# Sign of decoded weights by ScalarE, a first fold without group sum, and a first step in two halves, in a fused attention and expert kernel

## The chip, the cores and the metric

One core of a Trainium2 chip. The metric is the device time of one execution in microseconds, as a median of runs. All engines are named as in the profile: PE is TensorE, DVE VectorE, ACT ScalarE, POOL GpSimd, SP the queue that issues transfers.

## The reference

Causal attention (4 batches, 12 heads, 448 positions, head size 64), a soft mixture of 8 experts with 4 slots each, and a last feed-forward part of which this change touches the product:

```python
# x: 1792 tokens x 768, from the attention
c = softmax(x @ phi, axis=1)                 # 1792 x 32
x = c @ slot_out                             # slot_out: 32 x 768, from the experts
h = x @ w_in                                 # w_in: 768 x 2048
g = h * np.cos(h)
out = g @ w_out                              # w_out: 2048 x 768
```

`w_in` and `w_out` are float64 arrays; everything is computed in float32.

## The kernel before

Attention and experts come first, in orders written out by hand (HEAD, ORDER, TAIL and a loop over 48 pieces of expert weights, lines 799 to 857). Then the last part, which this document is about.

**Fold.** Since x = c @ slot_out, h is c @ (slot_out @ w_in). So `w_mm` (L868) multiplies the 32 slots with a chunk of 128 columns of `w_in`, in six products over the 768 rows (`soT`, the transposed slots, against the decoded item `fwi`). These six are spread over four groups of 32 rows of a PSUM bank, so that `w_4` (L884, ScalarE copy), `w_rep` (L887, a product with a 0/1 matrix that adds the four groups) and `w_s` (L890, ScalarE copy) follow. `w_d` (L894, VectorE) makes the residue for the low part, and the chunk lies in `WS`. GRP lists the chunks that are folded together: chunks 0 and 1 alone, the others in pairs.

**Steps.** A step is a block of tokens (three of 512, one of 256) and a chunk of 128 hidden columns: 64 steps, in the order of SEQ. Each runs `t_h` (H, TensorE product L910), `t_y` (Y, ScalarE, rounding to whole turns, L914), `t_r` (R, VectorE, L917), `t_s` (S, ScalarE, sine, L920), `t_g` (G, VectorE, times h, L923), `t_k` (K, ScalarE, the high part of g, L926) and `t_l` (L, the low part of g, on GpSimd, or on VectorE for the steps in LE, L929). Then come the products B that multiply g with `w_out`: six groups of three (high by high, high by low, low by high; `back`, L936 to L938), 12 products in the last block (`back3`, L964 to L966), and for step 0 in the order `back0` (L946): all six high by high, all six high by low, all six low by high.

**Decoding.** The float64 weights are loaded as pairs of 32-bit words, one item of 768 KB per chunk of `w_in` ("i") and `w_out` ("o"), 32 items; the words lie in four raw buffers. `dec_a` (L732, ScalarE) multiplies the high words, read as float32, by 2^-112, which moves the exponent; `dec_l` (L735, VectorE) shifts the low words right by 29; `dec_h` (L739, VectorE) shifts the high words left by 3 and ors them in, by which the sign falls out; `dec_s` (L743, VectorE) takes the sign bit from the high words and ors it in. For `w_out`, `up_part` (L754, ScalarE) and `lo_part` (L767, VectorE or GpSimd, by VE) split the item in a high and a low part. Three items are decoded in the expert part, by `next_piece` (L774), 29 by the planner's order.

**Order.** A planner (L994 to L1170) gives each operation a cost, what it depends on and a due time (`key`), and writes out one fixed order per engine. KEYS shifts the due times of single operations, LA says how long an engine may hold out for a more urgent one, and VE and LE fix the engine of some operations. It also puts filler products (`keep_warm`, L540) on TensorE while the chain to the first step runs.

In the expert part each piece's products are at L829 or L844, followed for some pieces by three filler products; after each group of four pieces a copy (L848), two transposes (L853, in `bank[6]`) and a copy to `soT` (L854).

Of the kernel before, what the change touches and what calls it, by code (L numbers as in the profile page):

```python
# [33 lines left out]
LA = 0.4  # L34
# [14 lines left out]
VE = {1: 'D', 10: 'P', 11: 'P', 12: 'P', 15: 'D', 6: 'P', 7: 'D'}  # L49
LE = {10: 'D', 11: 'D', 20: 'D', 25: 'D', 41: 'D', 47: 'D', 6: 'D', 8: 'D'}  # L50
# [152 lines left out]
def moe_stack_kernel(ctx: ExitStack, tc: tile.TileContext, qk, v, cst, phi, w1, w2, w_in, w_out, out):  # L203
# [526 lines left out]
    def dec_a(j):  # L730
        w = rawv(j)
        ACT.activation(w[:, :, 1].bitcast(F32), w[:, :, 1].bitcast(F32), AF.Copy, scale=2.0 ** -112)  # L732
# [4 lines left out]
    def dec_h(j):  # L737
        fi = it_f(j).bitcast(I32)
        DVE.scalar_tensor_tensor(fi, rawv(j)[:, :, 1], 3, fi, op0=ALU.logical_shift_left, op1=ALU.bitwise_or)  # L739

    def dec_s(j):
        fi = it_f(j).bitcast(I32)
        DVE.scalar_tensor_tensor(fi, rawv(j)[:, :, 1], -2147483648, fi, op0=ALU.bitwise_and, op1=ALU.bitwise_or)  # L743

    def decode(j):
        dec_a(j)
        dec_l(j)
        dec_h(j)
        dec_s(j)
# [20 lines left out]
    npc = [0]  # L770

# [27 lines left out]
    with tc.manual_schedule():  # L799
# [19 lines left out]
        for g in range(2):  # L819
# [17 lines left out]
            for n in range(3):  # L837
                sb = bank[4 + n % 2]
                for qd in range(4):
                    w = next_piece().rearrange("p (c j f) -> p c j f", c=2, j=4)  # L840
                    for c in range(2):
                        kc = 2 * qd + c
                        for j in range(4):
                            PE.matmul(sb[32 * j:32 * j + 4, 0:256], lhsT=hT[:, kc, 4 * j:4 * j + 4], rhs=w[:, c, j, :],  # L844
                                      start=(kc == 0), stop=(kc == 7))
                    if 42 <= npc[0] < 48:
                        keep_warm(3)
                ACT.activation(so, sb[:, 0:256], AF.Copy)  # L848
# [59 lines left out]
    def t_h(s, hb):  # L908
        blk, fc = seq[s][:2]
        PE.matmul(hb[:, 0:n_(s)], lhsT=WS[0:96, 128 * fc:128 * fc + 128], rhs=CT[:, TOK[blk]:TOK[blk + 1]], start=True, stop=True)  # L910

    def t_y(s, hb):

        ACT.activation(y_(s).bitcast(I32), hb[:, 0:n_(s)], AF.Identity, bias=b_q, scale=1.0 / (2.0 * math.pi))  # L914

    def t_r(s, hb):
        DVE.scalar_tensor_tensor(y_(s), y_(s).bitcast(I32), -2.0 * math.pi, hb[:, 0:n_(s)], op0=ALU.mult, op1=ALU.add)  # L917

    def t_s(s):
        ACT.activation(y_(s), y_(s), AF.Sin, bias=b_h, scale=1.0)  # L920

    def t_g(s, hb):
        DVE.tensor_tensor(y_(s), hb[:, 0:n_(s)], y_(s), ALU.mult)  # L923

    def t_k(s):
        ACT.activation(g_(s)[0], y_(s), AF.Copy)  # L926

    def t_l(s, eng):
        eng.tensor_tensor(g_(s)[1], y_(s), g_(s)[0].bitcast(F32), ALU.subtract)  # L929
# [70 lines left out]
    for j, (k_, c) in enumerate(items):  # L1000
# [3 lines left out]
        else:  # L1004
# [11 lines left out]
            task(("h", j), dict(D=.88), [("a", j), ("l", j)], key - 1.4, True)  # L1016
            task(("s", j), dict(D=.95), [("h", j)], key - 1.3, True)
# [7 lines left out]
    for q, grp in enumerate(GRP):  # L1025
        key = need[grp[0]] - 1.5
        n = len(grp)
        task(("wm", q), dict(T=.14 + .22 * (n + 1)), [("s", 2 * c) for c in grp] + [("w4", q - 2) if q >= 2 else None, ("so",)], key - .8)
        task(("w4", q), dict(A=.15 + .11 * n), [("wm", q)] + [("wr", q - 2) if q >= 2 else None], key - .7)
        task(("wr", q), dict(T=.1 + .22 * n), [("w4", q)], key - .6)  # L1030
        task(("ws", q), dict(A=.15 + .11 * n), [("wr", q)], key - .5)
# [6 lines left out]
    for s, (blk, fc, first, last) in enumerate(seq):  # L1038
        w = n_(s) / 512.0
        task(("H", s), dict(T=.02 + .22 * w), [("wd", qof[fc]), ("H", s - 1) if s else None], s - 3)  # L1040
        task(("Y", s), dict(A=.08 + .52 * w), [("H", s)] + [("K", s - 3), ("L", s - 3)] * (s >= 3), s - 2.6)
# [3 lines left out]
        task(("K", s), dict(A=.1 + .46 * w), [("G", s), ("B", s - 4, nu(s - 4) - 1) if s >= 4 else None], s - 1.7)  # L1045
        task(("L", s), dict(D=.07 + .55 * w) if LE.get(s) == "D" else dict(P=.07 + 1.3 * w), [("K", s)], s - 1.5, True)
        if s == 0:
            task(("B", 0, 0), dict(T=1.4), [("K", 0), ("u", 0)], .0)
            task(("B", 0, 1), dict(T=1.4), [("B", 0, 0), ("v", 0)], .1)
            task(("B", 0, 5), dict(T=1.4), [("B", 0, 1), ("L", 0)], .2)  # L1050
        for m in range(nu(s)):
            if s == 0:
                if last:
                    task(("F", s, m), dict(D=.61) if m % 2 == 0 else dict(A=.5), [("B", 0, 5)], s + .2 + m / 10)
                    pb[m] = ("F", s, m)
                continue
            pv_ = ("B", s, m - 1) if m else (("B", s - 1, nu(s - 1) - 1) if s else None)
            if blk == 3:
                task(("B", s, m), dict(T=(.68, .68, .73)[m]), [("K", s), ("L", s), ("u", fc), ("v", fc), pv_, *([pb.get(x) for x in ((0,), (2,), (1, 3))[m]] if first else [])], s + m / 10)
# [3 lines left out]
            task(("B", s, m), dict(T=.01 + .67 * w), [("K", s), ("L", s), ("u", fc), ("v", fc), pv_, pb.get(m) if first else None], s + m / 10)  # L1063
# [23 lines left out]
    CHN = [("wm", 0), ("w4", 0), ("wr", 0), ("ws", 0), ("wd", 0), ("H", 0), ("Y", 0), ("R", 0), ("S", 0), ("G", 0), ("K", 0), ("B", 0, 0)]  # L1087
# [24 lines left out]
    while len(done) < len(T):  # L1112
# [3 lines left out]
        for e in free:  # L1116
# [40 lines left out]
            if t[0] in ("G", "wd"):  # L1157
                hbf[hbo[("H" if t[0] == "G" else "wm", t[1])]] = fin + .1
# [9 lines left out]
        if not moved:  # L1168
# [4 lines left out]
    run = dict(ld=ld, a=dec_a, l=dec_l, h=dec_h, s=dec_s, u=up_part, S=t_s, K=t_k, B=lambda s, m: (back3 if seq[s][0] == 3 else back if s else back0)(s, m))  # L1173
    run.update(H=lambda s: t_h(s, bk(("H", s))), Y=lambda s: t_y(s, bk(("H", s))), R=lambda s: t_r(s, bk(("H", s))),
               G=lambda s: t_g(s, bk(("H", s))))
    for nm, fn in (("wm", w_mm), ("w4", w_4), ("wr", w_rep), ("ws", w_s), ("wd", w_d)):
        run[nm] = lambda q, fn=fn: fn(q, bk(("wm", q)))
    with tc.manual_schedule():
        for _, _, t, e in plan:
# [7 lines left out]
            elif t[0] == "L":  # L1187
                t_l(t[1], ENG[e])
# [68 lines left out]
```

## Time and profile before

| | us |
|---|---|
| median of 3 runs | 509.07 (507.99 to 509.58) |
| profiled execution | 508.61, its span 506.8 |
| TensorE busy | 479.2 (95% of the span) |
| VectorE busy | 361.6 (71%) |
| ScalarE busy | 306.7 (61%) |
| GpSimd busy | 176.3 (35%) |

The profile is of one execution. Busy times are of single engines; "idle before" of an instruction is the time in which its engine had nothing to run, with what ended it. TensorE's weight loads (PEld) overlap its products; a matmul's end is modelled, so the start times of two matmuls tell more than their durations.

### The profile page before, as it was taken

The page shows a single profiled execution, that of the slowest core. Times are in us where ns is not written, and L with a number is a line of the kernel's source. Part 1 is how long each engine was busy: PE and PEld are TensorE (multiplying, and loading weights), DVE is VectorE, ACT ScalarE, POOL GpSimd, SP SyncE. Part 2 cuts the span into 40 slices and gives each one's busy share as a digit, 9 for nine tenths or more (in the row PEclk, how much of TensorE's full clock was granted, in tenths as well). Part 3 has the DMA queues.
Part 4 walks back from the last instruction along what each step waited for, and adds up shares of the span by engine and source line. Part 5 has one row for each costly group of instructions (what it writes and reads, how often), then busy time and mean ns, then how long its engine had stood idle before and what let it go on. Part 6 is the DMA issues. An engine that isn't in the chain of part 4 may idle for free.

```text
span 506.8 us, 11358 instructions
## 1 busy us (share of the span) xinstructions
PE 479.2 (95%) x4304; PEld 345.1 (68%) x4304; DVE 361.6 (71%) x913; ACT 306.7 (61%) x734; POOL 176.3 (35%) x261
## 2 busy tenths in 40 slices
PE   8999999999998988788999999999999999999996
PEld 5766666666666333246777768777777878888885
DVE  4798889889885530054989999999979786455241
ACT  4998899899892210123877674567457565643361
POOL 2655555555551000000562132514327534312231
PEclk9999999999999999989999999999999999999999
DMA  6488888788867999998352542324252102023101
GB/s 202 121 289 294 285 296 310 276 291 307 292 239 281 407 420 415 423 420 352 124 188 62 188 147 104 117 94 163 63 174 78 58 4 94 32 80 120 51 0 63
DMA packets 23942, 100.38 MB, mean 198 GB/s; under 512 B 2768, under 2 KB 6352, under 8 KB 17744
## 3 DMA queue, kind: packets, MB, share of 16 engines
q1 hardware_dynamic: 23888, 99.66, 53.6%
q8 instruction: 34, 0.56, 0.4%
q14 instruction: 20, 0.16, 0.1%
HBM read 94.14 MB, written 5.51 MB: 197 GB/s over the span
## 4 chain that ended last, share of the span: by engine, by line
PE 40%; DVE 13%; DMA 11%; issue 3%; POOL 2%; ACT 2%; POOLq 0%; ACTq 0%; SPq 0%; DVEq 0%
DMA w<-in_w_dram 11%; PE bank L936 8%; PE bank L938 8%; PE bank L937 8%; PE bank L965 2%; PE bank L964 2%; PE bank L966 2%; PE bank L910 2%; DVE zscr L923 2%; PE bank L829 2%; DVE zfa L735 1%; POOL zg L929 1%; PE bank L540 1%; DVE zscr L917 1%; DVE zps L984 1%
## 5 line engine op out<-in xcount | busy, mean ns | idle before, releaser
L929 POOL TENSOR_TENSOR zg<-zscr,zg 128x512 fp32r<-128x512 f32 (+1 forms) x56 | 74.7, 1338 | 233.5 <-ACT zg L926 121.3
L936 PE MATMUL bank<-zg,zhl 128*128 128x512 f32 x282 | 112.2, 398 | 0.0
L938 PE MATMUL bank<-zg,zhl 128*128 128x512 f32 x282 | 110.3, 391 | 1.4 <-DVE zg L929 1.1
L937 PE MATMUL bank<-zg,zhl 128*128 128x512 f32 x282 | 110.1, 390 | 0.0
L360 ACT ACTIVATE p<-p,pst 128x192 f32<-128x192 f32 (+3 forms) x168 | 87.2, 521 | 14.6 <-DVE pst L358 14.1
L380 POOL TENSOR_SCALAR p<-p,pst 128x448 f32<-128x448 f32 (+3 forms) x123 | 66.4, 551 | 48.3 <-DVE pst L371 46.7
L917 DVE SCALAR_TENSOR_TENSOR zscr<-zscr,bank 128x512 f32<-128x512 int32 (+1 forms) x64 | 38.6, 615 | 34.5 <-ACT zscr L914 34.2
L938 PEld LDWEIGHTS bank<-zg,zhl 128*128 128x128 f32 x282 | 52.9, 188 | 14.0 <-DVE zg L929 1.5
L936 PEld LDWEIGHTS bank<-zg,zhl 128*128 128x128 f32 x282 | 53.0, 188 | 12.4 <-issue 1.2
L937 PEld LDWEIGHTS bank<-zg,zhl 128*128 128x128 f32 x282 | 53.1, 188 | 10.8
L920 ACT ACTIVATE zscr<-zscr,b_h 128x512 f32<-128x512 f32 (+1 forms) x64 | 41.7, 667 | 27.4 <-DVE zscr L917 26.6
L342 PE MATMUL bank<-qk 64*128 64x320 f32 (+2 forms) x288 | 57.5, 470 | 0.0
L914 ACT ACTIVATE zscr<-bank,b_q 128x512 int32<-128x512 f32 (+1 forms) x64 | 39.1, 629 | 28.6 <-PE bank L910 26.3
L358 DVE CUSTOM_DVE_ANT_0 p<-bank,cs 128x448 f32<-128x448 f32 (+1 forms) x96 | 51.7, 554 | 5.9 <-PE bank L342 5.6
L926 ACT ACTIVATE zg<-zscr 128x512 fp32r<-128x512 f32 (+1 forms) x64 | 36.7, 576 | 25.5 <-DVE zscr L923 17.3
L923 DVE TENSOR_TENSOR zscr<-bank,zscr 128x512 f32<-128x512 f32 (+1 forms) x64 | 39.1, 621 | 12.9 <-ACT zscr L920 12.8
L227 DVE COPY pts<-bank 128x512 f32<-128x512 f32 x47 | 32.1, 683 | 9.8 <-PE bank L387 9.0
L387 PE MATMUL bank<-cs,p 64*128 64x64 f32 (+1 forms) x768 | 34.7, 227 | 3.5 <-DVE p L382 2.0
L387 PEld LDWEIGHTS bank<-cs,p 64*128 64x128 f32 (+1 forms) x768 | 28.2, 133 | 12.4 <-ACT pts L225 7.1
L360 ACT ACTIVATION_READ_ACCUMULATOR p<-p,pst 128x1 f32 x168 | 31.8, 189 | 0.0
L732 ACT ACTIVATE zraw<-zraw 128x768 f32<-128x768 f32 x32 | 29.0, 908 | 1.9 <-DMA zraw<-in_w_out_dram 1.3
L225 ACT ACTIVATE pts<-bank 128x512 f32<-128x512 f32 x49 | 28.5, 582 | 2.3 <-PE bank L387 2.1
(169 smaller groups left out, 785.3 us busy)
## 6 DMA issues: line engine op xcount, KB each, us to landing
w<-in_w_dram SPq DMA_DIRECT2D x48, 1024.0 KB, 8.2
zraw<-in_w_in_dram SPq DMA_DIRECT2D x16, 768.0 KB, 4.4
zraw<-in_w_out_dram SPq DMA_DIRECT2D x16, 768.0 KB, 4.4
qk<-in_qk_dram SPq DMA_DIRECT2D x24, 480.0 KB, 4.0
xk<-in_v_dram SPq DMA_DIRECT2D x12, 256.0 KB, 4.1
out_dram<-zps SPq DMA_DIRECT2D x11, 256.0 KB, 2.1
xts<-in_v_dram SPq DMA_DIRECT2D x12, 128.0 KB, 4.3
lt<-in_v_dram SPq DMA_DIRECT2D x12, 128.0 KB, 4.3
```

The lines of the kernel that those rows point to most:

```text
L342: PE.matmul(sreg(j, c), lhsT=Q(p)[h, q0:q0 + 128], rhs=K(p)[h, 0:ln], start=True, stop=True)
L358: DVE.tensor_tensor_reduce(out=dst, in0=sb, in1=m, scale=-0.125, scalar=3.0e38, op0=ALU.add, op1=ALU.min, accum_out=st_[:, col:col + 1])
L360: return pr(f"exp{j}{c}")(lambda: ACT.activation(dst, dst, AF.Exp, bias=st_[:, col:col + 1], scale=-1.0, accum_out=st_[:, 8 + col:9 + col]))
L380: POOL.tensor_scalar(dst, dst, st_[:, 24 + col:25 + col], 0.0, op0=ALU.mult, op1=ALU.add)
L387: PE.transpose(out, src, by)
L917: DVE.scalar_tensor_tensor(y_(s), y_(s).bitcast(I32), -2.0 * math.pi, hb[:, 0:n_(s)], op0=ALU.mult, op1=ALU.add)
L920: ACT.activation(y_(s), y_(s), AF.Sin, bias=b_h, scale=1.0)
L923: DVE.tensor_tensor(y_(s), hb[:, 0:n_(s)], y_(s), ALU.mult)
L929: eng.tensor_tensor(g_(s)[1], y_(s), g_(s)[0].bitcast(F32), ALU.subtract)
L936: PE.matmul(o, lhsT=wh, rhs=gh, start=first, stop=False)
L937: PE.matmul(o, lhsT=wl, rhs=gh, start=False, stop=False)
L938: PE.matmul(o, lhsT=wh, rhs=gl, start=False, stop=last)
```

## The change

The sign now comes out of the rescaling: for negative words the factor is 2^-112 x 2^32, so that the exponent field holds one bit more, and the shift left by 3 moves that bit to where the sign is. The old `dec_h` goes by the name `dec_s`, and the old `dec_s` is gone. The fold of chunk 0 adds in three copies over all six products, so that it needs neither `w_4` nor `w_rep`; its first four blocks are multiplied after the second group of expert outputs of the last half, its last two at its old place. The transposes of the expert outputs go to `bank[7]`. Step 0 runs as two halves of 256 columns each. KEYS has other entries (some 70 instead of 60), LA is 0.5 instead of 0.4.

```diff
-VE = {1: 'D', 10: 'P', 11: 'P', 12: 'P', 15: 'D', 6: 'P', 7: 'D'}
-LE = {10: 'D', 11: 'D', 20: 'D', 25: 'D', 41: 'D', 47: 'D', 6: 'D', 8: 'D'}
+VE = {11: 'D', 13: 'D', 4: 'P'}
+LE = {1: 'D', 10: 'D', 11: 'D', 12: 'D', 13: 'D', 15: 'D', 16: 'D', 2: 'D', 23: 'D', 3: 'D', 30: 'D', 32: 'D', 39: 'D', 41: 'D', 42: 'D', 7: 'D', 9: 'D'}
...
-        ACT.activation(w[:, :, 1].bitcast(F32), w[:, :, 1].bitcast(F32), AF.Copy, scale=2.0 ** -112)
+        ACT.activation(w[:, :, 1].bitcast(F32), w[:, :, 1].bitcast(F32), AF.Prelu, scale=2.0 ** -112, alpha=2.0 ** 32)
...
-    def dec_h(j):
+    def dec_s(j):
         fi = it_f(j).bitcast(I32)
         DVE.scalar_tensor_tensor(fi, rawv(j)[:, :, 1], 3, fi, op0=ALU.logical_shift_left, op1=ALU.bitwise_or)
-
-    def dec_s(j):
-        fi = it_f(j).bitcast(I32)
-        DVE.scalar_tensor_tensor(fi, rawv(j)[:, :, 1], -2147483648, fi, op0=ALU.bitwise_and, op1=ALU.bitwise_or)
...
+    def w_first(c0, c1):
+        for ch in range(c0, c1):
+            for r in range(3):
+                PE.matmul(bank[6][32 * r:32 * r + 32, 256:384], lhsT=soT[:, ch, :],
+                          rhs=fwi(0)[:, 128 * ch:128 * ch + 128], start=(ch == 0), stop=(ch == 5))
...
-                tb = bank[6]
+                tb = bank[7]
...
+                if npc[0] == 44:
+                    w_first(0, 4)
...
+        if q == 0:
+            assert wb is bank[6] and GRP[0] == (0,)
+            w_first(4, 6)
+            return
...
+    def cr(s, u):
+        return slice(0, n_(s)) if s else slice(256 * u, 256 * u + 256)
...
+    def t_g(s, hb, u=0):
+        c = cr(s, u)
+        DVE.tensor_tensor(y_(s)[:, c], hb[:, c], y_(s)[:, c], ALU.mult)
...
-    CHN = [("wm", 0), ("w4", 0), ("wr", 0), ("ws", 0), ("wd", 0), ("H", 0), ("Y", 0), ("R", 0), ("S", 0), ("G", 0), ("K", 0), ("B", 0, 0)]
+    CHN = [("wm", 0), ("ws", 0), ("wd", 0), ("H", 0), ("Y", 0), ("R", 0), ("S", 0), ("G", 0), ("K", 0), ("B", 0, 0)]
```

The other operations of a step take the argument `u` in the same way as `t_g`, `back0` multiplies one half at a time, and the planner has tasks for both halves (`Hb` to `Lb` for the second). The costs that it reckons with for the rest are as before.

## Rows read from the trace of the kernel before

**Rows 1.** Stretch, its us, busy us of PE, PEld, DVE, ACT, POOL; clock, DMA
```profile
242.00:385.00 143.00, 138.39 (x715) 108.77 (x714) 134.22 (x173) 94.69 (x148) 54.39 (x32) 1.00 0.39 132
...
345.00:385.00 40.00, 38.65 (x207) 30.36 (x206) 34.45 (x45) 24.91 (x40) 17.88 (x11) 1.00 0.41 138
...
385.00:400.00 15.00, 15.00 (x67) 12.32 (x66) 13.18 (x21) 9.83 (x16) 7.91 (x5) 1.00 0.00 2
400.00:500.00 100.00, 100.00 (x506) 83.88 (x505) 52.08 (x89) 49.24 (x95) 31.61 (x31) 1.00 0.15 56
```
**Rows 2.** Waits of weight loads, 247 to 400 us: total us, times, longest
```profile
PEld bank L910 <- DVE zscr L923: 2.6, 4, 1.2
PEld bank L875 <- DVE zfa L743: 2.0, 2, 1.5
PEld bank L910 <- DVE zWS L896: 1.8, 3, 1.2
...
PEld bank L938 <- DVE zg L929: 1.5, 1, 1.5
...
PEld bank L938 <- POOL zg L929: 1.0, 2, 0.7
```
**Rows 3.** Timeline, 228 to 252 us: start us, us, engine, line, operation, operands
```profile
228.28 1.05 PE L844 MATMUL bank<-w,dk 128*4 128x256 f32 x16 [0.58 <-DMA w<-in_w_dram]
...
233.26 1.05 PE L844 MATMUL bank<-w,dk 128*4 128x256 f32 x16 [0.55 <-DMA w<-in_w_dram]
...
235.12 0.95 ACT L732 ACTIVATE zraw<-zraw 128x768 f32<-128x768 f32 x1 [0.31 <-DMA zraw<-in_w_out_dram]
...
235.68 1.07 PE L875 MATMUL bank<-zfa,dT 128*32 128x128 f32 x24
...
236.36 0.28 ACT L885 ACTIVATE cs<-bank 128x128 f32<-128x128 f32 x1 [0.29 <-PE bank L875]
...
237.19 0.27 ACT L892 ACTIVATE zWS<-bank 96x128 fp32r<-96x128 f32 x1
...
242.14 3.01 PE L946 MATMUL bank<-zg,zhl 128*128 128x512 f32 x12
...
245.42 0.94 DVE L767 TENSOR_TENSOR zhl<-lt,zhl 128x768 fp32r<-128x768 f32 x1
```
**Rows 4.** Operations by shape, 233 to 506.8 us: count, busy us, mean ns, idle before
```profile
L920 ACT ACTIVATE zscr<-zscr,b_h 128x512 f32<-128x512 f32 x48 | 33.8, 720 | 23.2 <-DVE zscr L917 23.0
L917 DVE SCALAR_TENSOR_TENSOR zscr<-zscr,bank 128x512 f32<-128x512 int32 x48 | 32.0, 680 | 12.6 <-ACT zscr L914 12.4
...
L926 ACT ACTIVATE zg<-zscr 128x512 fp32r<-128x512 f32 x48 | 30.1, 630 | 12.2 <-DVE zscr L923 11.5
...
L920 ACT ACTIVATE zscr<-zscr,b_h 128x256 f32<-128x256 f32 x16 | 7.9, 507 | 4.2 <-DVE zscr L917 3.6
...
L917 DVE SCALAR_TENSOR_TENSOR zscr<-zscr,bank 128x256 f32<-128x256 int32 x16 | 6.6, 420 | 21.9 <-ACT zscr L914 21.8
```
**Rows 5.** Timeline of TensorE near the end, one product of 512 columns, then 256
```profile
501.83 0.39 PE L966 MATMUL bank<-zhl,zg 128*128 128x512 f32 x1
...
502.06 0.28 PE L964 MATMUL bank<-zhl,zg 128*128 128x256 f32 x1
...
502.17 0.28 PE L965 MATMUL bank<-zhl,zg 128*128 128x256 f32 x1
```
**Rows 6.** Busy us, 242 to 385 us: L743 (DVE), then L929 (DVE, POOL)
```profile
242.00:385.00 143.00, 25.68 (x23) 1.00 0.39 132
...
242.00:385.00 143.00, 4.11 (x6) 39.58 (x24) 1.00 0.39 132
```
**Rows 7.** ScalarE's operations by line, 242 to 385 us
```profile
L732 ACT ACTIVATE zraw<-zraw 128x768 f32<-128x768 f32 x24 | 21.8, 907 | 1.6 <-DMA zraw<-in_w_out_dram 1.0 <-DMA zraw<-in_w_in_dram 0.5
```
**Rows 8.** ScalarE's table loads by line, whole span
```profile
L360 ACT ACT_TABLE_LOAD x1 | 1.3, 1283 | 0.7 <-PEq L1242 0.7
L655 ACT ACT_TABLE_LOAD x1 | 1.3, 1283 | 0.0
```

More of the change, by code (lines that the diff above doesn't have):

```diff
@@ L33 @@
 SAFE = 0.0
-LA = 0.4
+LA = 0.5
 KD = 0.0
@@ L747, in decode @@
         dec_l(j)
-        dec_h(j)
         dec_s(j)
@@ L906, in g_, with t_h, t_y, t_r @@
         return [ar[f"g{(k + u) // 4}"][:, ((k + u) % 4) * 512:((k + u) % 4) * 512 + n_(s)] for u in range(2)]
-    def t_h(s, hb):
+    def cr(s, u):
+        return slice(0, n_(s)) if s else slice(256 * u, 256 * u + 256)
+    def t_h(s, hb, u=0):
         blk, fc = seq[s][:2]
[L910 to L929, printed above, removed]
+        c = cr(s, u)
+        PE.matmul(hb[:, c], lhsT=WS[0:96, 128 * fc:128 * fc + 128], rhs=CT[:, TOK[blk] + c.start:TOK[blk] + c.stop], start=True, stop=True)
+    def t_y(s, hb, u=0):
+        c = cr(s, u)
+        ACT.activation(y_(s)[:, c].bitcast(I32), hb[:, c], AF.Identity, bias=b_q, scale=1.0 / (2.0 * math.pi))
+    def t_r(s, hb, u=0):
+        c = cr(s, u)
+        DVE.scalar_tensor_tensor(y_(s)[:, c], y_(s)[:, c].bitcast(I32), -2.0 * math.pi, hb[:, c], op0=ALU.mult, op1=ALU.add)
+    def t_s(s, u=0):
+        c = cr(s, u)
+        ACT.activation(y_(s)[:, c], y_(s)[:, c], AF.Sin, bias=b_h, scale=1.0)
+    def t_g(s, hb, u=0):
+        c = cr(s, u)
+        DVE.tensor_tensor(y_(s)[:, c], hb[:, c], y_(s)[:, c], ALU.mult)
+    def t_k(s, u=0):
+        c = cr(s, u)
+        ACT.activation(g_(s)[0][:, c], y_(s)[:, c], AF.Copy)
+    def t_l(s, eng, u=0):
+        c = cr(s, u)
+        eng.tensor_tensor(g_(s)[1][:, c], y_(s)[:, c], g_(s)[0][:, c].bitcast(F32), ALU.subtract)
     def back(s, m):
@@ L940, in back0 @@
     def back0(s, m):
-        k_ = (0, 1, None, None, None, 2)[m]
+        k_, u = m % 10, m // 10
+        c = cr(0, u)
         gh, gl = g_(0)
@@ L945, in back0 @@
             fc = seq[0][1]
-            PE.matmul(bank[m][:, 0:n_(0)], lhsT=w_blk(fc, int(k_ == 1), m), rhs=gl if k_ == 2 else gh, start=k_ == 0,
+            PE.matmul(bank[m][:, c], lhsT=w_blk(fc, int(k_ == 1), m), rhs=(gl if k_ == 2 else gh)[:, c], start=not (k_ or u),
                       stop=k_ == 2 and seq[0][3])
@@ L1015, in moe_stack_kernel @@
             task(("l", j), dict(D=.48), d + fr, key - 1.5, True)
-            task(("h", j), dict(D=.88), [("a", j), ("l", j)], key - 1.4, True)
-            task(("s", j), dict(D=.95), [("h", j)], key - 1.3, True)
+            task(("s", j), dict(D=.95), [("a", j), ("l", j)], key - 1.4, True)
         if k_ == "o" and c < NEW // 2:
@@ L1027, in moe_stack_kernel @@
         n = len(grp)
[L1028 to L1031, printed above, removed]
+        if q == 0:
+            task(("wm", 0), dict(T=.5), [("s", 0), ("so",)], key - .8)
+        else:
+            task(("wm", q), dict(T=.14 + .22 * (n + 1)), [("s", 2 * c) for c in grp] + [("w4", q - 2) if q > 2 else None, ("so",)], key - .8)
+            task(("w4", q), dict(A=.15 + .11 * n), [("wm", q)] + [("wr", q - 2) if q > 2 else None], key - .7)
+            task(("wr", q), dict(T=.1 + .22 * n), [("w4", q)], key - .6)
+        task(("ws", q), dict(A=.15 + .11 * n), [("wr", q) if q else ("wm", q)], key - .5)
         task(("wd", q), dict(D=.17 + .13 * n), [("ws", q)], key - .4)
@@ L1039, in moe_stack_kernel @@
         w = n_(s) / 512.0
-        task(("H", s), dict(T=.02 + .22 * w), [("wd", qof[fc]), ("H", s - 1) if s else None], s - 3)
-        task(("Y", s), dict(A=.08 + .52 * w), [("H", s)] + [("K", s - 3), ("L", s - 3)] * (s >= 3), s - 2.6)
+        if s == 0:
+            w = .5
+            for u, x in enumerate(("", "b")):
+                o = [("wd", qof[fc])]
+                for nm, e, dur, key in (("H", "T", .02 + .22 * w, -3), ("Y", "A", .08 + .52 * w, -2.6), ("R", "D", .07 + .54 * w, -2.5),
+                                        ("S", "A", .1 + .56 * w, -2.4), ("G", "D", .07 + .54 * w, -2.3), ("K", "A", .1 + .46 * w, -1.7)):
+                    task((nm + x, s), {e: dur}, o + [(nm, 0)] * (u and nm == "H"), key + .01 * u)
+                    o = [(nm + x, s)]
+                task(("L" + x, s), dict(D=.07 + .55 * w) if LE.get(s) == "D" else dict(P=.07 + 1.3 * w), o, -1.5 + .01 * u, True)
+                task(("B", 0, 10 * u), dict(T=.7), [("K" + x, 0), ("u", 0)] + [("B", 0, 0)] * u, .05 * u)
+                task(("B", 0, 10 * u + 1), dict(T=.7), [("B", 0, 10 * u), ("v", 0)], .1 + .05 * u)
+                task(("B", 0, 10 * u + 2), dict(T=.7), [("B", 0, 10 * u + 1), ("L" + x, 0)], .2 + .05 * u)
+            continue
+        task(("H", s), dict(T=.02 + .22 * w), [("wd", qof[fc]), ("H", s - 1) if s > 1 else ("Hb", 0)], s - 3)
+        task(("Y", s), dict(A=.08 + .52 * w), [("H", s)] + ([("K", s - 3), ("L", s - 3)] if s > 3 else [("Kb", 0), ("Lb", 0), ("L", 0)] * (s == 3)), s - 2.6)
         task(("R", s), dict(D=.07 + .54 * w), [("Y", s)], s - 2.5)
@@ L1044, in moe_stack_kernel @@
         task(("G", s), dict(D=.07 + .54 * w), [("S", s)], s - 2.3)
-        task(("K", s), dict(A=.1 + .46 * w), [("G", s), ("B", s - 4, nu(s - 4) - 1) if s >= 4 else None], s - 1.7)
+        task(("K", s), dict(A=.1 + .46 * w), [("G", s), *([("B", s - 4, nu(s - 4) - 1)] if s > 4 else [("B", 0, 2), ("B", 0, 12)] * (s == 4))], s - 1.7)
         task(("L", s), dict(D=.07 + .55 * w) if LE.get(s) == "D" else dict(P=.07 + 1.3 * w), [("K", s)], s - 1.5, True)
[L1047 to L1050, printed above, removed]
         for m in range(nu(s)):
[L1052 to L1057, printed above, removed]
+            pv_ = [("B", s, m - 1)] if m else ([("B", s - 1, nu(s - 1) - 1)] if s > 1 else [("B", 0, 2), ("B", 0, 12)])
             if blk == 3:
-                task(("B", s, m), dict(T=(.68, .68, .73)[m]), [("K", s), ("L", s), ("u", fc), ("v", fc), pv_, *([pb.get(x) for x in ((0,), (2,), (1, 3))[m]] if first else [])], s + m / 10)
+                task(("B", s, m), dict(T=(.68, .68, .73)[m]), [("K", s), ("L", s), ("u", fc), ("v", fc), *pv_, *([pb.get(x) for x in ((0,), (2,), (1, 3))[m]] if first else [])], s + m / 10)
                 if last:
@@ L1062, in moe_stack_kernel @@
                 continue
-            task(("B", s, m), dict(T=.01 + .67 * w), [("K", s), ("L", s), ("u", fc), ("v", fc), pv_, pb.get(m) if first else None], s + m / 10)
+            task(("B", s, m), dict(T=.01 + .67 * w), [("K", s), ("L", s), ("u", fc), ("v", fc), *pv_, pb.get(m) if first else None], s + m / 10)
             if last:
@@ L1156, in moe_stack_kernel @@
                 hbf[b], hbo[t] = 1e9, b
-            if t[0] in ("G", "wd"):
-                hbf[hbo[("H" if t[0] == "G" else "wm", t[1])]] = fin + .1
+            if t[0] in ("G", "wd") and t != ("G", 0) or t == ("Gb", 0):
+                hbf[hbo[("wm" if t[0] == "wd" else "H", t[1])]] = fin + .1
             pool.remove(t)
@@ L1172, in moe_stack_kernel @@
     bk = lambda t: bank[6 + hbo[t]]
-    run = dict(ld=ld, a=dec_a, l=dec_l, h=dec_h, s=dec_s, u=up_part, S=t_s, K=t_k, B=lambda s, m: (back3 if seq[s][0] == 3 else back if s else back0)(s, m))
+    run = dict(ld=ld, a=dec_a, l=dec_l, s=dec_s, u=up_part, S=t_s, K=t_k, B=lambda s, m: (back3 if seq[s][0] == 3 else back if s else back0)(s, m))
     run.update(H=lambda s: t_h(s, bk(("H", s))), Y=lambda s: t_y(s, bk(("H", s))), R=lambda s: t_r(s, bk(("H", s))),
                G=lambda s: t_g(s, bk(("H", s))))
+    run.update(Hb=lambda s: t_h(s, bk(("H", s)), 1), Yb=lambda s: t_y(s, bk(("H", s)), 1), Rb=lambda s: t_r(s, bk(("H", s)), 1),
+               Sb=lambda s: t_s(s, 1), Gb=lambda s: t_g(s, bk(("H", s)), 1), Kb=lambda s: t_k(s, 1))
     for nm, fn in (("wm", w_mm), ("w4", w_4), ("wr", w_rep), ("ws", w_s), ("wd", w_d)):
@@ L1186, in moe_stack_kernel @@
                 lo_part(t[1], ENG[e])
-            elif t[0] == "L":
-                t_l(t[1], ENG[e])
+            elif t[0] in ("L", "Lb"):
+                t_l(t[1], ENG[e], len(t[0]) - 1)
             elif t[0] == "F":
```

24 rows, old and new, of the table KEYS are left out of this document.

## The prediction

> **What bounds the kernel now.** I read the busy times by stretch first, then what TensorE waited for, then the timeline of the start, and last the costs of single operations.
>
> The kernel has three parts: attention (up to about 166 us), the expert part, in which TensorE waits for weight loads (up to 233 us), and the last product, which is the only one that the change touches. In the last part TensorE is the bound: from 400 to 500 us it is busy 100.00 of 100 us while VectorE has 52.08 us of work. From 242 to 385 us it is not quite the bound: it is busy 138.39 of 143 us, and VectorE 134.22 (94%), ScalarE 94.69 (66%), GpSimd 54.39 [rows 1]. The 4.6 us of idle TensorE understate the loss, because modelled matmul ends cover part of each gap. The waits of its weight loads tell it better: between 247 and 400 us they waited 2.6 + 2.0 + 1.8 + 1.5 us for VectorE results and 1.0 us for GpSimd ones, 8.9 us in 12 waits [rows 2]. Between two loads that nothing holds up there is also a small gap: matmuls of 512 columns start 0.23 us apart [rows 5] and a load takes 0.19, so 0.04 us of each wait is no loss. 8.9 - 12 x 0.04 leaves **8.4 us lost to late data**. In the 15 us from 385 to 400 VectorE was still busy 13.18 (88%), and TensorE lost nothing; in the 40 us before, at 34.45 (86%), TensorE was idle 1.35 [rows 1], but its 2.0 us of waits there were for the sign operation L743 itself [rows 2]. So I read the loss as that of a VectorE without slack, in whose line late results stand behind decoding.
>
> The other loss is the start. The last expert weights land and their products begin at 233.26; the first product of the first step starts at 242.14 [rows 3]. Between lies a chain of small operations, one after the other, in which TensorE only runs its filler products.
>
> **The change, part by part.**
>
> *Sign by ScalarE.* Per decoded weight item one VectorE operation goes, the sign operation of L743. From 242 to 385 us that is 23 of them, 25.68 us [rows 6], 1.12 us each. The other shift-and-or stays as it is. ScalarE runs the same number of operations: L732 now takes 907 ns for 768 elements per partition [rows 7]. The trace has no leaky function. It can't be cheaper, as the elements stay the same; the nearest dearer form is a function whose bias is read from memory, 720 against 630 ns for a plain copy at equal size [rows 4]. So 0 to 0.09 us each, at most 24 x 0.09 = 2.2 us, and I take 0: ScalarE has 48 us idle in the stretch [rows 1]. That cover would have to be gone before it counts. The 32-bit word buffers come free one operation earlier, so SP issues their reloads about 1 us earlier. I cost that at nothing: the item that ScalarE waited for until 235.12 landed after the last expert weights, whose products begin at 233.26 [rows 3], so these transfers stand in line behind the weights and displace nothing.
>
> *More residues on VectorE.* The table LE names 17 steps instead of 8. Of those whose turn falls before 385 us, by my count of steps (the 30 steps that ScalarE starts there), 14 instead of 6 are VectorE's: 8 more at 0.685 us (4.11 / 6 [rows 6]), plus 5.5 us. GpSimd is rid of 8 at 1.65 (39.58 / 24 [rows 6]).
>
> VectorE then has 134.2 - 25.7 + 5.5 = 114.0 us of work. The stretch would shrink to some 137 us, which makes 83%, below the 88% at which nothing was lost [rows 1]. What of the 8.4 us goes? If the loss fell in a straight line from 94% to nothing at 52%, 83% would still lose 6.2 us; by the 385 to 400 us stretch it would lose nothing. That stretch is the nearer row, as it has the same mix of decoding and steps, but it is short, and the order of the work has other weights throughout, whose effect no row shows. So I leave a third, 2.8 us, and take **minus 5.6**. The ends are minus 2.2 and minus 8.4. What is late next: the last of a chain of five operations between VectorE and ScalarE, no longer queued behind decoding.
>
> *First fold without its group sum.* Before, ScalarE copies the four partial sums at 236.36, TensorE adds them, and ScalarE's next copy follows at 237.19 [rows 3]. After, the 12 last instructions of the fold write the full sum in three copies, as many instructions as the 12 that the copy at 236.36 waited for, and the later copy comes at once. That removes 237.19 - 236.36 = **0.83 us** of the chain. What it adds, 24 instructions for four of the six blocks, goes ahead, after the second group of expert outputs. Its price is that of the 24 at 235.68, 1.07 us [rows 3]. It is hidden by waiting for weights: of the three batches that follow, the first waited 0.58 us for its transfer and the last 0.55, 1.13 together [rows 3]. With that cover gone it would delay the start by up to 1.07 us. Its transposes move to another bank; nothing waits for that.
>
> *First step in two halves.* The chain to the first product has three ScalarE and two VectorE operations and a product, now at half length. ScalarE: 720 to 507 ns, saves 0.21, taken for all three; VectorE: 680 to 420, saves 0.26, for both [rows 4]; the product: 0.23 to about 0.115 apart [rows 5], 0.12. Together 3 x 0.21 + 2 x 0.26 + 0.12 = **1.27 us**. The second halves fit into the pauses, since each engine alternates with the other. The price on TensorE: 36 products at 0.115 to 0.12 instead of 18 at 0.23 [rows 5], plus one load more: 0.2 us at most. There is a second price. Step 1 must be ready about 2 us sooner. Its weights depend on the item of 235.12, whose low part VectorE computed at 245.42 [rows 3], the last thing that step 1 needed. Without the sign operation it could be done by about 239.5 (four operations at 0.95 us, the length of the two shown, and hand-overs), but VectorE has a residue of 0.685 us and 0.3 us of halves more in these 9 us. The unknown is 0 to 2.1 us, all of the gain; I take 0.5, nearer to nothing because the item's removed sign operation gives 1.1 us back there.
>
> **Sum.** -0.83 - 1.27 + 0.2 + 0.5 - 5.6 = **-7.0 us**. The profiled execution took 508.61 us, its span 506.8; that is 0.46 below the median of the runs, 509.07, and from the median I get **502.1 us**. The end does not change: the last products and the transfer out are the same.
>
> **Rivals.**
>
> *The waits stay and change their name.* The engines run in a fixed order. If what was late was the order, not VectorE's load, then removing work moves the wait to the next operation in the chain. For it: the waits are on five different results [rows 2], and the idle share of TensorE is the same at 86% as over the whole stretch, 1.35 of 40 against 4.6 of 143 [rows 1]. Against it: TensorE idles nowhere from 385 to 500 us [rows 1], with the same chains. It would keep the start, -1.4, and up to a third of the 8.4: 505 to 507.7; if step 1 takes the whole start gain back as well, 509. Chance 0.27.
>
> *Table switches.* If the leaky function were not in the set of functions that the sine needs, each decoding step would load its table and the sine would load its own again. A load is 1.283 us [rows 8], two per item 2.57, and 24 items 61.6 us on top of ScalarE's 94.69 [rows 1]: 156 us of work in a stretch of 143. ScalarE becomes the bound, at least 13 us longer, and with the start gained about **520 us**, more where each switch also stands in the five-operation chain. It decides once about 19 of the 24 items cost two loads (48 us idle / 2.57). For it: the function is new here. Against it: the kernel's copies, relu and identity run beside exp and sine with two loads in all, one per set [rows 8]. Chance 0.06.
>
> The Trainium skill, page "ScalarE: Activation LUTs", section "Table sets: the hidden batching unit", says that functions come in sets, that cheap ones such as relu and copy are in every set, and that a switch costs about 2.7 us with its drain, which would put this rival at 24 x 2 x 2.7 = 130 us of ScalarE work as an estimate by that page. It does not list the leaky one; the trace agrees on the cheap ones and shows 1.283 us for the load alone.
>
> **How the numbers follow.** The forecast, most of the late-data loss gone: 498.9 to 505.0, chance 0.67. The chain rival 0.27, of which 0.10 lands within 0.3% (1.5 us, about what a measurement of this kernel tells from no change) and 0.01 above. Table switches 0.06. Faster 0.83, same 0.10, slower 0.07. The low end is everything gone at its bound: 509.07 - 2.1 + 0.2 - 8.4 = 498.8, and a little below for the run's spread: 498.5. The high end, 506.5, takes in half of the chain rival; the forecast's own range lies inside.
>
> **What would show it.** Right: no sign operation; 32 ScalarE rescalings of about 0.91 us and still two table loads; the first product of step 0 some 8.9 - 2.1 = 6.8 us after the last weights' products begin; VectorE near 83% in the stretch that ends with the decoding; the waits of weight loads for VectorE and GpSimd results near 3 us. The fold's step is wrong if the three batches of expert products before the end start late. The forecast is wrong if VectorE has slack and the waits still sum to 6 us or more, or if ScalarE shows table loads.

## The result and the profile after

The changed kernel took 501.9 us (501.48 to 503.06), the kernel before beside it 509.07 (507.99 to 510.0): a ratio of 0.9868 [0.9847, 0.989], 7.2 us less. The profiled execution took 502.82. The busy times of its page:

```profile
span 501.0 us, 11371 instructions
...
PE 478.5 (95%) x4329; PEld 346.2 (69%) x4329; DVE 331.0 (66%) x896; ACT 307.8 (61%) x736; POOL 152.1 (30%) x249
```

VectorE has 30.6 us less work, ScalarE 1.1 us more. The stretches of [rows 1] (us; busy PE, PEld, DVE, ACT, POOL; clock, DMA):

```profile
242.00:385.00 143.00, 142.46 (x756) 115.05 (x756) 123.05 (x179) 105.35 (x165) 41.68 (x28) 1.00 0.39 135
...
385.00:400.00 15.00, 15.00 (x88) 12.04 (x87) 8.43 (x14) 8.26 (x14) 5.38 (x4) 1.00 0.00 1
```

TensorE is busy 142.46 instead of 138.39 us, and VectorE is down from 94% to 86%. The waits of weight loads for VectorE results from 247 to 400 us, as in [rows 2] (total us, times, longest); there is none for GpSimd:

```profile
...
PEld bank L923 <- DVE zscr L939: 0.9, 1, 0.9
PEld bank L956 <- DVE zg L947: 0.4, 1, 0.4
PEld bank L884 <- DVE zfb L741: 0.4, 1, 0.4
PEld bank L884 <- DVE uacc L737: 0.4, 1, 0.4
PEld bank L923 <- DVE zWS L905: 0.2, 1, 0.2
```

That is 2.3 us in 5 waits where there were 8.9 in 12, or 2.3 - 5 x 0.04 = 2.1 us lost where there were 8.4. The start, from the timeline, as in [rows 3]:

```profile
234.71 1.05 PE L847 MATMUL bank<-w,dk 128*4 128x256 f32 x16 [0.58 <-DMA w<-in_w_dram]
...
237.83 0.27 ACT L901 ACTIVATE zWS<-bank 96x128 fp32r<-96x128 f32 x1 [0.32 <-PE bank L772]
...
238.48 0.51 PE L923 MATMUL bank<-CT,zWS 96*128 96x256 f32 x2
...
239.02 0.84 ACT L927 ACTIVATE zscr<-bank,b_q 128x256 int32<-128x256 f32 x2 [0.45 <-PE bank L923]
...
239.89 0.75 DVE L931 SCALAR_TENSOR_TENSOR zscr<-zscr,bank 128x256 f32<-128x256 int32 x2 [0.48 <-ACT zscr L927]
...
240.35 0.91 ACT L935 ACTIVATE zscr<-zscr,b_h 128x256 f32<-128x256 f32 x2 [0.33 <-DVE zscr L931]
...
242.14 4.48 PE L965 MATMUL bank<-zg,zhl 128*128 128x256 f32 x36
...
246.80 0.19 PEld L954 LDWEIGHTS bank<-zg,zhl 128*128 128x128 f32 x1 [0.27 <-ACT zg L943]
...
247.61 0.19 PEld L956 LDWEIGHTS bank<-zg,zhl 128*128 128x128 f32 x1 [0.42 <-DVE zg L947]
```

The fold now goes straight from its products to the copy at 237.83. The first product of step 0 starts 242.14 - 234.71 = 7.43 us after the last expert products do (8.88 before). ScalarE's lines:

```profile
L734 ACT ACTIVATE zraw<-zraw 128x768 f32<-128x768 f32 x32 | 28.3, 902 | 1.6 <-DMA zraw<-in_w_out_dram 1.3 <-DMA zraw<-in_w_in_dram 0.2
...
L362 ACT ACT_TABLE_LOAD x1 | 1.3, 1283 | 0.7 <-PEq L1269 0.7
L657 ACT ACT_TABLE_LOAD x1 | 1.3, 1283 | 0.0
```

The leaky rescaling takes 902 ns, the plain one took 907 [rows 7], and there are two table loads as before.

**How the runs are compared.** The last expert products start at 233.26 us in the profile of before and at 234.71 in that of after, with the same transfers ahead of them. So 1.45 us lie in a part that the change hardly touches (of its edits only the fold's four early blocks lie there), which is as much as its edits at the start are worth. I therefore give two further figures of each profile: the **chain** (first product of step 0 minus start of the last expert products) and the **last part** (span minus start of the last expert products). A second execution of after gave 7.44 and 266.38 against 7.43 and 266.29, so the last part repeats within 0.1 us between these two profiles. The ratios are to executions of before beside each run.

| kernel | median us | ratio to before [95%] | last expert products | chain | last part |
|---|---|---|---|---|---|
| before | 509.07 | | 233.26 | 8.88 | 273.54 |
| after | 501.90 | 0.9868 [0.9847, 0.989] | 234.71 | 7.43 | 266.29 |
| e1_sign_back | 525.79 | 1.0353 [1.0328, 1.0378] | 233.53 | 7.98 | 289.17 |
| e2_before_nosign | 505.12 | 0.9935 [0.992, 0.995] | 235.28 | 8.88 | 267.92 |
| e3_sign_half | 509.89 | 1.0037 [1.0024, 1.0049] | 233.59 | 7.97 | 274.41 |
| e4_keys_before | 507.32 | 0.9974 [0.9962, 0.9986] | 233.76 | 7.21 | 271.44 |
| e5_before_all | 502.63 | 0.9881 [0.9863, 0.9899] | 233.48 | 8.71 | 267.72 |
| e6_split0 | 501.30 | 0.9846 [0.9829, 0.9862] | 233.98 | 6.88 | 265.92 |
| e7_whole0 | 501.38 | 0.9854 [0.984, 0.9869] | 233.33 | 7.92 | 266.47 |
| e8_old_fold | 502.02 | 0.9865 [0.9851, 0.988] | 233.56 | 8.02 | 267.04 |
| e9_step1 | 502.02 | 0.9869 [0.9846, 0.9893] | 233.94 | 6.88 | 266.56 |
| e10_le_before | 502.10 | 0.9868 [0.9844, 0.9892] | 235.02 | 7.44 | 266.48 |
| e11_no_keys | 501.30 | 0.9849 [0.9829, 0.9868] | 233.18 | 7.22 | 266.22 |
| e12_after | 502.58 | 0.9875 [0.9851, 0.9898] | 235.82 | 7.44 | 266.38 |

The last part fell by 273.54 - 266.29 = 7.25 us, the medians by 7.17: the whole gain lies there, 1.45 of it in the chain and 5.80 behind it. The medians of e5 to e12 (501.30 to 502.63) are not told apart from after's own two (501.90, 502.58), so what is said of the edits in these runs rests on one profile each.

### The profile page after: what moved, and what is told of

It is laid out like the page before. It is cut to its first block, busy times and chain, and to the rows that moved or that the text cites. A ratio compares the mean times of both kernels' runs of the same rounds, so it can differ in the third digit from the quotient of the medians.

```text
span 501.0 us, 11371 instructions
## 1 busy us (share of the span) xinstructions
PE 478.5 (95%) x4329; PEld 346.2 (69%) x4329; DVE 331.0 (66%) x896; ACT 307.8 (61%) x736; POOL 152.1 (30%) x249
## 4 chain that ended last, share of the span: by engine, by line
PE 55%; DMA 11%; DVE 3%; ACT 1%; issue 0%; SPq 0%; ACTq 0%
PE bank L954 13%; PE bank L956 13%; PE bank L955 13%; DMA w<-in_w_dram 11%; PE bank L923 3%; PE bank L984 2%; PE bank L983 2%; PE bank L985 2%; PE bank L832 2%; PE bank L884 1%; PE bank L433 1%; PE bank L542 1%; PE bank L897 1%; DVE zscr L931 1%; DVE zscr L939 0%; DVE lt L741 0%
## 5 line engine op out<-in xcount | busy, mean ns | idle before, releaser
L947 POOL TENSOR_TENSOR zg<-zscr,zg 128x512 fp32r<-128x512 f32 (+1 forms) x48 | 56.3, 1179 | 263.0 <-ACT zg L943 219.3
```

Of the source, the lines that this page charges most:

```text
L947: eng.tensor_tensor(g_(s)[1][:, c], y_(s)[:, c], g_(s)[0][:, c].bitcast(F32), ALU.subtract)
```

## The experiments

Theory A is the prediction's: the loss is that of a VectorE without slack, and each edit at the start is worth what it takes out of the chain. Theory B is its first rival: the loss is that of a fixed order that does not fit its operations, and the order decides.

**Sign put back, in the order of after (e1), and for `w_out` alone (e3).**

```diff
-        ... AF.Prelu, scale=2.0 ** -112, alpha=2.0 ** 32)
+        ... AF.Copy, scale=2.0 ** -112)
...
+        DVE.scalar_tensor_tensor(fi, rawv(j)[:, :, 1], -2147483648, fi, op0=ALU.bitwise_and, op1=ALU.bitwise_or)
```

e3 has the same edit under `if j % 2`, and keeps the leaky function for the even items.

> The changed kernel in its own order, with the plain rescaling and the sign operation put back right behind each shift-and-or. Theory A (the loss was a VectorE without slack): from 240 to 380 us VectorE has 121.4 of 140 us of work after the change, and 23 or 24 operations of 1.12 us make it 147, more than the stretch holds, so at least 7 us come back: 508 to 512 us, and the waits of weight loads for VectorE results sum to 8 us or more. Theory B (the new order of the work did it): the order is kept, so at most 2 us come back: 502 to 504.

> As the first, but the sign operation comes back only for the w_out items, 12 or so of them between 240 and 380 us, 13 us of VectorE work: 134 to 135 of 140 us, 96%, as full as the kernel before was. Theory A: a loss like that of the kernel before, which lost 8.4 us at 94%, so 3 to 7 us back: 505 to 509. If the loss grows only with work that does not fit: 0 to 1 us, 502 to 503. Theory B: at most 1 us.

Measured: e1 is 289.17 - 266.29 = 22.9 us longer than after in the last part, e3 8.1 us. The stretch and the largest waits (247 to 400 us) of e1:

```profile
242.00:385.00 143.00, 126.08 (x658) 98.00 (x660) 134.96 (x180) 93.08 (x146) 39.04 (x26) 0.99 0.39 130
```

```profile
PEld bank L924 <- DVE zWS L906: 9.9, 5, 3.5
PEld bank L924 <- DVE zscr L940: 7.2, 5, 2.8
```

VectorE is as full as before, 134.96 against 134.22 of 143 us [rows 1] (365.3 against 361.6 us over the whole span), yet TensorE is idle 16.9 us instead of 4.6. What is late is the fold's residue and the factor of a step. So a full VectorE loses time, as A says, but nearly the same load loses several times as much in an order that has no place for the operation, which A does not say: e1 lies far above the range of either theory. e3, with 14 of the operations in the stretch, is as full (133.82), and its last part is nearly that of before (274.41 against 273.54): 1 us above A's range, and far above B's.

**Sign taken away, in the order of before (e2).**

```diff
-        ... AF.Copy, scale=2.0 ** -112)
+        ... AF.Prelu, scale=2.0 ** -112, alpha=2.0 ** 32)
...
     def dec_s(j):
-        fi = it_f(j).bitcast(I32)
-        DVE.scalar_tensor_tensor(fi, rawv(j)[:, :, 1], -2147483648, fi, op0=ALU.bitwise_and, op1=ALU.bitwise_or)
+        pass
```

> The kernel before in its own order, with the leaky rescaling and without the sign operation; fold, first step, weights of the order and engines of the residues are those of before. Theory A: VectorE falls to about 108.5 of 143 us, the late data go from 8.4 us to 2 to 3: 503 to 504 us. Theory B: the fixed order keeps its waits: 507 to 509.

Measured: the last part falls from 273.54 to 267.92, **5.62 us**, with the chain at 8.88 as before. The median falls by 3.4 us only; in the profiled execution the part ahead ended 2.0 us later than in before's (235.28 against 233.26). The stretch, and the waits for data from 247 to 400 us that are longer than 0.4 us:

```profile
242.00:385.00 143.00, 142.46 (x749) 114.12 (x748) 114.22 (x158) 99.91 (x157) 52.80 (x34) 1.00 0.39 130
```

```profile
PEld bank L909 <- DVE zscr L922: 1.5, 4, 0.6
...
PEld bank L937 <- POOL zg L928: 0.7, 1, 0.7
```

TensorE is busy 142.46 us, the same as in after. Nothing else of the change is in this kernel, and the waits did not take another name. This is A's result.

**The due times of before, with all else of after (e4), and none at all (e11).**

```diff
-LA = 0.5
+LA = 0.4
...
-    ('B', 10, 2): 5.5, ('B', 12, 4): 3.5, ('B', 18, 1): 1, ('B', 2, 4): -3.5, ('B', 20, 0): 4, ('B', 20, 4): 2,
...
+    ('B', 10, 3): -4, ('B', 10, 4): 4.75, ('B', 11, 5): 13.25, ('B', 12, 3): 4, ('B', 14, 0): 0.5, ('B', 14, 3): -2,
...
```

VE and LE are those of before too. In e11 the only edit is `KEYS = {}`.

> The changed kernel with the due-time shifts, engine choices and hold-out share (KEYS, VE, LE, LA) of the kernel before, so the planner writes another order for the new operations. Theory A: VectorE has slack in any order: 501.5 to 504. Theory B (the order did it): 505 or more.

> The changed kernel with no shift of a due time at all, its engine choices kept. The shifts of the kernel before gave 507.3 us with these operations. If those were only unfit, no shifts at all give less: 502 to 504.5. If any order that was not fitted loses the same, 506 to 508.

Measured: e4 271.44, 5.2 us longer than after; e11 266.22, the same as after. The stretch and the three largest waits for data (247 to 400 us) of e4, then the stretch of e11:

```profile
242.00:385.00 143.00, 138.84 (x731) 110.60 (x730) 114.71 (x165) 102.41 (x160) 56.06 (x36) 1.00 0.39 134
```

```profile
PEld bank L921 <- DVE zWS L903: 2.6, 3, 1.8
PEld bank L882 <- DVE zfb L739: 1.4, 1, 1.4
PEld bank L882 <- DVE zscr L937: 1.3, 1, 1.3
```

```profile
242.00:385.00 143.00, 142.37 (x753) 115.13 (x752) 121.61 (x179) 104.53 (x164) 42.89 (x28) 1.00 0.38 133
```

In e4 VectorE has 114.71 us of work, 80%, less than in after (86%), and TensorE still idles 4.2 us, where e2, just as full (114.22), idles 0.5: B's mechanism, real at a load that A called harmless. In e11 the planner's own due times do as well as the 70 shifts, so the new shifts bring nothing that these runs can tell. The old shifts with the old LA, VE and LE, made for other operations, cost 5.2 us together. Which of them cost it was not separated.

**All edits in the order of before (e5).** The kernel is e2 with the fold and the halves added, each second half right behind the first:

```diff
+    def w_first(c0, c1):
...
+        if q == 0:
+            w_first(4, 6)
+            return
...
+    def both(f):
+        def go(s, *a):
+            for u in range(1 if s else 2):
+                f(s, *a, u)
+        return go
...
+    run.update(H=lambda s: both(t_h)(s, bk(("H", s))), Y=lambda s: both(t_y)(s, bk(("H", s))),
...
```

> The order, due-time shifts and engine choices of the kernel before, with all three edits written into their places: leaky rescaling and no sign operation, the fold of chunk 0 in three sums with four blocks ahead, step 0 in halves one behind the other. The run with the rescaling alone shortened the part from the last expert products' begin to the end of the span by 5.6 us (273.5 to 267.9). Theory A (the edits do it all): 266 to 267 us for that part, as in the changed kernel (266.3). Theory B (the new order of the work carries the start): the start gains nothing, 267.5 to 268.

Measured: the chain is 8.71 (e2: 8.88), the last part 267.72 (267.92). Its timeline ahead of the first product:

```profile
239.13 2.84 PE L540 MATMUL bank<-cs 128*128 128x128 f32 x24
...
241.33 0.72 ACT L949 ACTIVATE zg<-zscr 128x256 fp32r<-128x256 f32 x2
...
242.04 0.39 PE L540 MATMUL bank<-cs 128*128 128x128 f32 x2
242.19 1.55 PE L971 MATMUL bank<-zg,zhl 128*128 128x256 f32 x11
```

The fixed order still gives TensorE 26 filler products there, the last of which start 0.15 us before the first product, and the halves run as pairs. In the old order the start's edits are worth 0.2 us: here B is right.

**The first step whole (e7), the old fold (e8), the engines of the residues (e10), each alone undone in after.**

```diff
-        return slice(0, n_(s)) if s else slice(256 * u, 256 * u + 256)
+        return slice(0, n_(s))
...
-            if t in TIMED:
+            if t in TIMED or t[0] in ("Hb", "Yb", "Rb", "Sb", "Gb", "Kb", "Lb") or t[0] == "B" and t[1] == 0 and t[2] >= 10:
                 continue
```

```diff
-                if npc[0] == 44:
-                    w_first(0, 4)
...
-            assert wb is bank[6] and GRP[0] == (0,)
-            w_first(4, 6)
-            return
+            pass
...
     def w_s(q, wb):
+        if q == 0:
+            w_4(0, wb)
+            w_rep(0, wb)
```

```diff
-                t_l(t[1], ENG[e], len(t[0]) - 1)
+                t_l(t[1], DVE if t[1] in (6, 8, 10, 11, 20, 25, 41, 47) else POOL, len(t[0]) - 1)
```

> The changed kernel with step 0 whole, in the places of the first halves. By the prediction's step the first product comes 1.27 us later; if the halves were held together at the rounding, less: 0.6 to 0.8. The part from the last expert products to the end grows as much if the chain decides, by less than 0.3 us if step 1 decides.

> The changed kernel with the old fold of chunk 0: six products over four row groups in the old place, copy, group sum, copy, one behind the other. By the prediction's step the first product comes 0.83 us later, and no product of the expert part is delayed any more. The part to the end grows by 0.83 if the chain decides, by less than 0.3 if step 1 decides.

> The changed kernel with the residues of the 8 steps that the kernel before named on VectorE, and all others on GpSimd, in their places of the order. By the prediction VectorE is freed of 5.5 us and GpSimd gets 13 us more. If VectorE's load decides, the time stays or falls by up to 0.5 us; if an order that does not reckon with the longer GpSimd operations decides, 2 us or more come back: 504 or above.

Measured: e7 lengthens the chain by 7.92 - 7.43 = 0.49 us and the last part by 0.18; e8 the chain by 0.59 and the last part by 0.75; e10 the last part by 0.19, hardly more than it repeats. From e7's timeline the products of step 0, and the stretch of e10:

```profile
241.25 4.37 PE L965 MATMUL bank<-zg,zhl 128*128 128x512 f32 x18 [0.16 <-ACT zg L943]
```

```profile
242.00:385.00 143.00, 142.37 (x759) 115.37 (x758) 119.45 (x173) 105.98 (x166) 52.98 (x35) 1.00 0.41 137
```

The fold is worth 0.59 to 0.75 of the 0.83 that were priced. The halves are worth much less than their price, and their 36 products take 0.11 us longer than the 18 (4.48 against 4.37). The residues' engine moves work (VectorE 119.45 instead of 123.05 us) but no time.

**The halves separated (e6).** In the timeline of after VectorE's first R starts at 239.89, 0.87 us behind the start of the two Y's at 239.02, which take 0.84: it waits for both. Not every pair is held so: the first S starts at 240.35, before the second R ends (239.89 + 0.75 = 240.64). H, Y and R use the PSUM bank that the two halves share, S does not. e6 gives the second half a bank of its own and puts its product behind the group sum of chunk 1.

```diff
     def t_h(s, hb, u=0):
+        hb = bank[5] if u else hb
...
+    order = [x[2:] for x in plan]
+    i = [x[0] for x in order].index(("Hb", 0))
+    x = order.pop(i)
+    i = [y[0] for y in order].index(("wr", 1))
+    order.insert(i + 1, x)
...
-        for _, _, t, e in plan:
+        for t, e in order:
```

> The changed kernel, with the second half's product of step 0 in a bank of its own and behind the group sum of chunk 1, by which the first half's rounding no longer waits for both halves. In the trace of the changed kernel the first VectorE operation of step 0 starts at 239.89, just as the second half's rounding ends. Expected: the first product of step 0 comes 0.4 to 0.6 us sooner after the last expert products than 7.43 us. If the chain to the first product decides, the time falls as much; if step 1 decides (its first product waited for ScalarE, its third for VectorE), by 0 to 0.1.

Measured: chain 6.88 (by 0.55 shorter), last part 265.92 (by 0.37). Its timeline:

```profile
237.75 0.39 PE L924 MATMUL bank<-CT,zWS 96*128 96x256 f32 x1
...
238.17 0.84 ACT L929 ACTIVATE zscr<-bank,b_q 128x256 int32<-128x256 f32 x2 [0.33 <-PE bank L924]
...
238.71 0.75 DVE L934 SCALAR_TENSOR_TENSOR zscr<-zscr,bank 128x256 f32<-128x256 int32 x2
...
240.86 4.48 PE L969 MATMUL bank<-zg,zhl 128*128 128x256 f32 x36
```

R now starts 0.54 us behind Y, while the second half is still being rounded; that is 0.33 of the chain's 0.55. Y starts 0.42 us behind the first H product, where it was 0.54 (238.48 to 239.02 in after), another 0.12. e6 makes two edits at once. Of the programs built with one of them each, neither of which was run, the one with the second bank alone has the separate waits, and the one with the moved product alone does not: with a shared bank the first Y waits for the second product, and the first R for the second Y. Whole against separated halves is 266.47 - 265.92 = 0.55 us. Some of the chain's gain goes to waits at step 1. By the last part this is the best version, but its median of 501.30 is not told apart from after's 501.90 and 502.58.

**Step 1 sooner (e9).** On top of e6, the operations of step 1 go ahead of those of step 2 on all engines:

```diff
+    mv = [("l", 4), ("H", 2), ("Kb", 0), ("B", 0, 0), ("Y", 1), ("L", 0), ("B", 0, 10), ("R", 1), ("u", 1),
...
+    order[at:at + len(mv)] = [(t, part_[t]) for t in mv]
```

In this kernel step 3's product is written to its bank before step 2 reads its factor there, so step 2 works on step 3's values; the operations are the same in kind and number. But step 2 has to wait for that product, so the run shows what step 1's waits are worth only roughly.

> The run with step 0's halves in two banks, and in addition step 1's operations ahead of step 2's on ScalarE and VectorE, with chunk 1's high and low part between them. In that run step 1's first product waited 0.4 us for ScalarE and its third 0.4 for VectorE. If step 1 decides the start, both waits go and the part from the last expert products' begin to the end falls from 265.9 to 265.2 or 265.4 us; if step 2 or the decoding behind them becomes late, it does not fall. Time 500.5 to 501.3.

Measured: chain 6.88, last part 266.56, 0.64 longer than e6. The first product of step 1 and the largest wait for data from 244 to 400 us:

```profile
245.38 0.39 PE L958 MATMUL bank<-zg,zhl 128*128 128x512 f32 x1
```

```profile
PEld bank L884 <- DVE zfb L741: 1.0, 1, 1.0
```

Step 1's waits are gone, and the decoding behind it is late instead: the wait for `zfb` is 1.0 us, and was 0.4 in e6. What the start gains there comes back in the next place, in this order.

**After once more (e12)**, with no edit:

> The changed kernel again, on the same chip as the others, for comparison: 501.5 to 502.5 us.

Measured: 502.58, the last part 266.38. This is the measure for the table above.

## Why the prediction was right, and where not

**The time.** The forecast was 502.1, the median 501.9. By parts: -5.6 for the sign, measured -5.62 in e2; -1.4 for the start with step 1's lateness, measured 266.29 - 267.92 = -1.63 between e2 and after, with whatever the new order brings by itself. That the terms fit so closely is in part luck: the 2.8 us left for the sign were a guess between two ends (-2.2 and -8.4), and the start has a term that was mis-sized (the halves, below).

**The sign.** The size holds, as do 2.1 us left of 2.8 and the waits (2.3 us for "near 3"). The reason given holds by half. That removing the operation frees the late chains without any new order is shown by e2. That the load of VectorE alone tells the loss is refuted: at 94% the loss is 8.4 us in before and over twice that in e1, and at 80% TensorE idles 4.2 us in e4 and 0.5 in e2. "So I read the loss as that of a VectorE without slack" should have been: slack makes an order forgiving, it does not replace one. The chain rival is right where an order was made for other operations. VectorE came to 86%, not 83%: 123.05 us, where 114.0 were forecast. The residues and low parts (L947 and L764) take 18.5 us of it, against 9.4 before (L929 and L767) and 5.5 priced on top; most of the rest is that more steps and output blocks fall into the same 143 us. The decoding is not it: its two shifts (L737 and L741) take 46.4 us for 28 items, and took 46.8 for 23.

**The fold.** -0.83 of the chain was priced; e8 shows 0.59 in the chain and 0.75 in the last part. The four blocks multiplied early lie ahead of the last expert products, so neither figure holds their price. The prediction's sign against the fold, three batches that start late, is there in after's profile: 230.37, 232.22 and 234.71 against 228.28, 230.79 and 233.26. But most of that delay is older than the early blocks (see the last section), and in eight other profiles with this fold the last batch starts between 233.18 and 233.98. In after's profile the cover held for the last batch, which waits 0.58 us for its transfer, 0.55 before [rows 3]. In e12, the same kernel, the last batch waits for none:

```profile
235.82 1.05 PE L847 MATMUL bank<-w,dk 128*4 128x256 f32 x16
```

Where the part ahead is that late, the cover is gone, and what the early blocks cost there no run shows.

**The halves.** This step failed. -1.27 was priced, with "each engine alternates with the other", and 0.49 in the chain and 0.18 in the last part were measured (e7). The engines did not alternate on H, Y and R, where the second half was waited for as well, which by the programs built for e6 comes from the shared bank; separated (e6), the chain came to 6.88, next to the 6.8 forecast. The total of the start fits all the same, and that is not explained: undone one at a time, the fold and the halves account for 0.75 + 0.18 = 0.93 of 1.63 us. The other 0.7 may need both edits together, or come from the new order without either; the edits in the old order bring 0.2 in all (e5), and after with both undone was not run.

**The small terms.** TensorE +0.2: measured 0.11. Step 1 late +0.5: the waits at 246.80 and 247.61 are 0.27 + 0.42 = 0.69 us. The leaky function at 0: 902 against 907 ns. More residues on VectorE: no time (e10).

**Table switches.** Two loads in all: this rival is out. "ScalarE: Activation LUTs" of the Trainium skill, section "Table sets: the hidden batching unit", does not list the leaky function among the cheap ones of every set; this trace shows it beside the sine without a load.

## What to carry to other kernels

Where a second engine is nearly as full as the bounding one, taking operations off it is worth the waits that stand against it, here 5.6 us for 29 operations of 1.1 us. But test the edit once in the old order and once with the order's adjustments cleared, since adjustments made for other operations can cost nearly as much as the edit brings (5.2 us here). When a chain is cut in halves, look in the trace whether the consumer of the first half starts before the second half's producer has ended; here the halves needed a PSUM bank each.

## What the runs showed that I had not expected

**The part ahead varies more than the edits at the start are worth.** With nearly the same attention and expert work in all kernels, the last expert products start between 233.18 and 235.82 us. Most of the difference is there when the expert part begins. In after, e2, e10 and e12 its first product starts between 167.42 and 167.95 us, and the last ones at 234.71 or later; in the ten other profiles the first starts between 166.17 and 166.84 and the last ones between 233.18 and 233.98. From the timelines of after, e11 and e2:

```profile
167.42 5.16 PE L832 MATMUL bank<-w,phs 128*4 128x512 f32 x36
```

```profile
166.23 4.05 PE L819 MATMUL bank<-w,phs 128*4 128x512 f32 x36
```

```profile
167.93 2.33 PE L828 MATMUL bank<-w,phs 128*4 128x512 f32 x20
```

After and e11 differ only in the order of the last part. They also differ in the clock granted from 166 to 170 us:

```profile
166.00:170.00 4.00, 3.95 (x22) 1.66 (x26) 3.08 (x8) 0.63 (x1) 0.00 (x0) 0.57 0.99 416
```

```profile
166.00:170.00 4.00, 4.00 (x39) 1.08 (x41) 3.10 (x7) 0.63 (x1) 0.00 (x0) 1.00 1.03 422
```

The first is after, at 0.57 (most of it at the lower level, 1.2 GHz), the second e11, at 1.00 (2.4 GHz): the first 36 expert products take 5.16 us against 4.05, behind a stretch (160 to 166 us) in which TensorE was busy 5.12 and 5.07 of 6 us. In the second profile of after, e12, the clock is 0.62 there. The clock is not needed for a late part ahead, as e2 has 1.00 there and its last expert products at 235.28. What delays the attention in these four profiles was not looked into.

**Two halves in one bank acted as one.** The first R started 0.87 us behind the first Y in after and 0.54 in e6, the first Y 0.54 us behind the first product and 0.42: together 0.45 of the 0.55 us by which the chain fell. S, which does not touch the shared bank, was not held so: it starts before the second R ends.
